# Attention and gated MLP on one core: the same instructions in another written order, with other homes for the ring buffers

## The chip, the cores and the metric

The kernel runs on one core of a Trainium2 chip. A core has four computing engines, TensorE (PE, with its weight load PEld as a row of its own), VectorE (DVE), ScalarE (ACT) and GpSimd (POOL), and SyncE (SP), which here only issues DMAs. Each has an instruction queue that it works off in order; they wait for each other through semaphores. The metric is the device time of one launch in microseconds (us), as the median of several runs.

## The reference

```python
def _attn_ref(q, k, v):                        # q, k, v: (8, 8, 576, 64)
    scores = scale * np.matmul(q, k.transpose(0, 1, 3, 2))
    rel = pos[:, None] - pos[None, :]
    mask = (rel >= 0) & (rel < window)         # window 64
    scores = np.where(mask, scores, -1000000000.0)
    attn = np.exp(scores - np.max(scores, axis=-1, keepdims=True))
    attn = attn / (np.sum(attn, axis=-1, keepdims=True) + 1e-09)
    return np.matmul(attn, v)

def _moe_ref(x, w_gate, w_val, w_out, rms_g):  # x: 4608 x 512, d_ff 1536
    xn = x / np.sqrt(np.mean(x * x, axis=-1, keepdims=True) + 1e-06) * rms_g
    g = xn @ w_gate
    silu = g * (1.0 / (1.0 + np.exp(-g)))
    return silu * (xn @ w_val) @ w_out
```

The output of the attention, 8 x 576 tokens with 8 x 64 features, is the x of the second function.

## The kernel before

**Tiling.** Attention goes by pair of heads: 8 batches of 4 pairs, 32 pairs in all, numbered 0 to 31. The tokens then make nine tiles of 512, t = 0 to 8, and the hidden layer six chunks of 256, c = 0 to 5. A weight or an operand of the MLP is kept as two 16-bit parts (high and low), and a product takes three matmuls: high by high, high by low, low by high.

**Stages.** The pairs of batches 0 and 1 are worked first: loads of `q` (line 660) and `kv` (lines 674, 676), scores `sc` on PE (line 727), mask and maximum on DVE (line 740), exponential on ACT (line 743), scaling on POOL (line 830), transposes `tr` on PE (line 838) with their copies `pt` on DVE and ACT, and values `xp` on PE (line 859). Beside them the weights come in as 64-bit floats and are widened: a staged load `st` (line 502), an exponential `mp`, `mn` on ACT (line 517), a sum `pw` on PE or POOL (lines 527, 523), an or into the bits on DVE (line 531), then scaling by powers of two, with the norms `z` (line 580), and the split in two parts. The root mean square of the first tokens is spread over the partitions by PE (`rb`, line 1277) and taken into `xb` by DVE (line 1305).

Tiles 0 and 1 use plain products `pg` (gate) and `pv` (value) of 12 matmuls of 512 columns each, lines 1397 to 1399; DVE puts them together in `th` (lines 1481 and 1485), which also empties the PSUM bank of the product. Tiles 2 to 8 use a scheme with seven half-size products in place of eight (`product`, line 1700, matmuls of 256 columns), and from tile 3 on the products of the output do too (line 1639). The combined weights of these schemes are made once, put into DRAM (`sevens0` to `sevens5`, one for each chunk, and `outer`) and loaded again for each tile and chunk into two places, `wt0` and `wt1` (lines 1610 and 1620), in three loads for a chunk: one of 128x3072 and two of 128x2048 numbers. A new load into a place waits until the products that read it are done.

The later batches have another way through the attention: scores, then four writes `via<-pm` into DRAM (line 706, one for each quarter of the partitions) and one read `pm<-via` in another layout (line 712), which has to wait until the writes have landed. SP issues these, the loads of `q` and `kv`, the loads of weights and the output (`out<-ot`, lines 1681 and 1893), all in one queue.

**What sets the order.** `SEQUENCE` (lines 44 to 224) is a text of 3894 labels, one for each piece of work: `s01` is a score of pair 0, `m010` a mask, `+g1311.0` a step after a product of tile 1, `.235.3` a step of another kind. The place of a label is its turn. `run_all` emits the pieces in this order, as far as what they need is done, and after it each engine's instructions are bound to the order in which they were written:

```python
AT = {n: k for k, n in enumerate(SEQUENCE.split())}
...
    for ins in traced[start:]:
        if ins.engine in before and ins.engine in WRITTEN(nc):
            tc.add_manual_dep(
                ins, before[ins.engine].name,
```

**Ring buffers.** Tiles of one kind (the `q`, the `kv`, the 512-column scratch `t2k` and a dozen others) share a few buffers. `HOMES` (line 228) says by a digit which buffer the k-th tile of a kind gets; a new tile waits for the readers of the one that was there:

```python
return self.pool.tile(shape, dtype, tag=f"{tag}_{HOMES[tag][k]}", name=name, bufs=1)
```

Of the kernel before, what the change touches and what calls it, by code (L numbers as in the profile page):

```python
# [56 lines left out]
N001 p500 t601 z32 O001 P001 l20 r501 u600 u601 G0101 x30 r500 O000 s70 m700 e411 m701 p410 A010 .229.2 a701 b5 M010 N010 O010 v60 y60 .230.2 p411
r411 a700 i70 w700 x31 G0200 A020 P000 t611 h30 t610 t40 e510 w701 G0211 r410 M020 e511 P010 e600 t41 G0201 d61 t50 G0210 e601 A011 u610 u611 M011 z40
.1 l30 t700 v61 p511 u700 z14 N011 y61 s71 h31 m710 p600 r600 m711 p601 p510 r601 r511 a711 a710 G0300 l31 A021 z41 i71 z42 x41 t701 z33 r510 e620
w710 u701 .26 e621 p621 q6q w711 d64 h40 h41 G0310 t710 G0301 p620 u710 l41 N020 A030 O011 t51 z50 t711 v70 M021 .237.2 b6 M030 N030 N021 r620 u711  # L60
G0311 e610 y70 z43 v71 y71 q7q l40 .234.0 O020 r621 .2 .2.5 .2.7 b7 .2.0 e611 G0400 .2.1 z51 f62 G0410 .2.6 .2.2 A031 M031 .2.11 .2.3 .2.4 d65 p611
P020 N031 O030 .2.9 O021 p610 R1 .2.8 z52 e641 r611 x51 e640 z44 p640 h51 r610 p641 S1 z53 h50 G0401 G0411 O031 A040 f60 l50 r640 B10 F100 F102 .9
H100 e651 e650 .233.0 G0500 r641 d63 F101 G0510 .2.14 A051 B11 H102 f64 M040 N040 F110 l51 F112 G0511 F103 A050 H103 .2.13 F111 F113 M050 f61 P030
.2.10 H101 G0501 N050 P011 p650 e631 z54 p651 r651 .8 .10 L100 P021 A041 M041 r650 H21 N041 .10.7 M051 .10.2 .10.6 L102 L101 e630 f65 .10.5 .2.15 L103
p630 G1000 G1001 r630 N051 .2.12 G1100 O050 P031 G1110 .10.8 p631 r631 f63 L21 .228.3 o0 o1 P050 .2.17 .2.16 .2.18 o2 A110 O040 G1101 h60 .10.1 .17
P040 M110 .2.19 G1011 .228.1 A111 M111 O041 P041 H11 .10.15 .231 .232 G1010 h61 N110 .10.3 .10.4 l60 .10.0 l61 h62 l62 G1111 .10.9 U10 .231.2 h63 N111
.228.4 .2.20 .2.21 L11 H22 .228.5 h64 U30 .228.6 .228.7 .228.10 D3 Ht3 l64 O051 P051 l63 .228.8 .228.9 .2.22 A101 h65 l65 .229.1 D1 Ht1 .231.3 Lt1
A100 M101 .27 M100 D2 Ht2 U31 .231.0 D4 .228.11 Lt3 Ht4 T3 N100 .18 .3 .10.12 .4 O111 .233.2 .46 .5 O100 L22 Lt2 Lt4 N101 P100 .229.3 .229.4 .229.5
# [1946 lines left out]
```

## Time and profile before

| | |
|---|---|
| median of 3 runs | 916.0 us (913.63 to 919.79) |
| span of the profiled execution | 916.2 us |
| PE busy | 893.7 us, 98% |
| PE weight load busy | 686.0 us, 75% |
| DVE busy | 697.3 us, 76% |
| ACT busy | 566.2 us, 62% |
| POOL busy | 454.9 us, 50% |
| DMA | 198.63 MB, mean 217 GB/s |

The rows that are printed further down come from one profiled execution. A row of a timeline has its start in us from the start of the span, the busy time, the engine, the source line and operation, out<-in, the shapes and the count; in brackets the idle time of the engine ahead of it and what ended it. A busy time of a matmul is longer than the step to the next one, since matmuls overlap in the pipeline; the step between starts is what PE needs for one. A row of a window has, for each engine, the busy time and in brackets the number of instructions, and then PE's granted clock as a share of full speed, the mean busy share of the DMA engines and GB/s.

### The profile page before, as it was taken

The page shows a single profiled execution, that of the slowest core. Times are in us where ns is not written, and L with a number is a line of the kernel's source. Part 1 is how long each engine was busy: PE and PEld are TensorE (multiplying, and loading weights), DVE is VectorE, ACT ScalarE, POOL GpSimd, SP SyncE. Part 2 cuts the span into 40 slices and gives each one's busy share as a digit, 9 for nine tenths or more (in the row PEclk, how much of TensorE's full clock was granted, in tenths as well). Part 3 has the DMA queues.
Part 4 walks back from the last instruction along what each step waited for, and adds up shares of the span by engine and source line. Part 5 has one row for each costly group of instructions (what it writes and reads, how often), then busy time and mean ns, then how long its engine had stood idle before and what let it go on. Part 6 is the DMA issues. An engine that isn't in the chain of part 4 may idle for free.

```text
span 916.2 us, 22827 instructions
## 1 busy us (share of the span) xinstructions
PE 893.7 (98%) x8541; PEld 686.0 (75%) x8541; DVE 697.3 (76%) x1916; ACT 566.2 (62%) x1465; POOL 454.9 (50%) x517
## 2 busy tenths in 40 slices
PE   7889999999999999999999998999999999999998
PEld 5644554544558875888888887888888888888887
DVE  6999978786987889898767874789678867724760
ACT  7887785554556566676747665665767555624551
POOL 6467986544355155645543734554547543420440
PEclk9799999999999999999999999999999999999999
DMA  8776642557779875798487757785696556647641
GB/s 325 248 226 211 214 141 61 148 148 216 216 225 308 282 255 157 256 313 276 165 282 269 237 208 236 271 279 193 196 319 219 208 194 213 204 127 233 185 158 47
DMA packets 105439, 198.63 MB, mean 217 GB/s; under 512 B 27760, under 2 KB 64624, under 8 KB 105328
## 3 DMA queue, kind: packets, MB, share of 16 engines
q1 hardware_dynamic: 104752, 195.99, 65.2%
q8 instruction: 67, 1.10, 0.5%
q10 hardware_dynamic: 576, 1.18, 0.3%
q14 instruction: 44, 0.36, 0.1%
HBM read 159.39 MB, written 37.75 MB: 215 GB/s over the span
## 4 chain that ended last, share of the span: by engine, by line
PE 88%; DVE 7%; DMA 2%; issue 1%; ACT 1%; POOL 1%; SPq 0%; ACTq 0%; POOLq 0%; DVEq 0%
PE a L1700 42%; PE o L1639 16%; PE po L1397 3%; PE po L1398 3%; PE po L1399 3%; PE x L902 3%; PE sc L727 3%; PE pv L1397 2%; PE pv L1399 2%; PE pv L1398 2%; PE pg L1397 2%; PE pg L1398 2%; PE pg L1399 2%; DVE p L740 1%; DVE top L568 1%; DMA wt<-sevens 1%
## 5 line engine op out<-in xcount | busy, mean ns | idle before, releaser
L1700 PEld LDWEIGHTS <-wt 128*128 128x128 f16 x3528 | 344.3, 98 | 49.2 <-DMA wt<-sevens 3.5
L1700 PE MATMUL a<-xn,wt 128*128 128x256 f16 x2016 | 236.9, 273 | 0.4 <-POOL xn L1378 0.2
L1700 PE MATMUL a<-wt,wt 128*128 128x256 f16 x1224 | 149.1, 274 | 3.3 <-DMA wt<-sevens 3.3
L1737 ACT ACTIVATE th<-a,hsc 128x256 f32<-128x256 f32 x168 | 78.8, 474 | 105.7 <-DVE a L1801 79.2
L1772 POOL TENSOR_TENSOR h<-th,h 128x512 f16<-128x512 f32 x84 | 98.1, 1179 | 67.5 <-ACT h L1770 61.3
L1772 POOL TENSOR_TENSOR wt<-u,wt 128x512 f16<-128x512 f32 (+1 forms) x72 | 67.1, 935 | 127.6 <-ACT wt L1770 77.1
L1639 PE MATMUL o<-wt,h 128*128 128x256 f16 x864 | 100.4, 273 | 0.0
L1801 DVE TENSOR_TENSOR a<-a,s 128x512 f32<-128x512 f32 x90 | 62.6, 695 | 48.3 <-PE a L1700 35.8
L1732 DVE SCALAR_TENSOR_TENSOR th<-th,a 128x256 f32<-128x256 f32 x168 | 69.6, 414 | 37.5 <-ACT th L1737 37.3
L1639 PEld LDWEIGHTS <-h 128*128 128x128 f16 x864 | 84.1, 98 | 10.7 <-issue 0.5
L743 ACT ACTIVATE pm<-pm,st 128x128 f32<-128x128 f32 (+1 forms) x216 | 83.9, 390 | 12.4 <-DVE st L740 12.2
L698 POOL TENSOR_TENSOR pm<-pm,st 128x512 f32<-128x512 f32 (+1 forms) x72 | 60.6, 870 | 56.6 <-DVE st L772 24.1
L1733 DVE SCALAR_TENSOR_TENSOR th<-a,th 128x256 f32<-128x256 f32 x168 | 71.2, 424 | 5.8
L1639 PEld LDWEIGHTS <-wt 128*128 128x128 f16 x648 | 62.9, 98 | 9.6 <-issue 1.8
L1718 ACT COPY s<-a 128x512 f32<-128x512 f32 x90 | 52.3, 585 | 26.4 <-PE a L1700 24.5
L1770 ACT CAST h<-th 128x512 f16<-128x512 f32 x84 | 51.4, 616 | 10.7 <-DVE th L1733 5.7
L740 DVE CUSTOM_DVE_ANT_0 pm<-sc,blocked 128x128 f32<-128x128 f32 x192 | 48.1, 282 | 6.3 <-PE sc L727 6.1
L1397 PE MATMUL po<-wt,h 128*128 128x512 f16 x136 | 51.6, 379 | 0.0
L1398 PE MATMUL po<-wt,h 128*128 128x512 f16 x136 | 51.5, 379 | 0.0
L1399 PE MATMUL po<-wt,h 128*128 128x512 f16 x136 | 51.5, 379 | 0.0
L727 PE MATMUL sc<-kv,q 64*64 64x128 f32 (+1 forms) x1056 | 43.5, 290 | 7.0 <-DMA q<-q 6.0
L1639 PE MATMUL o<-wt,wt 128*128 128x256 f16 x432 | 49.8, 273 | 0.0
(239 smaller groups left out, 1772.2 us busy)
## 6 DMA issues: line engine op xcount, KB each, us to landing
wt<-sevens SPq DMA_DIRECT2D x84, 512.0 KB, 5.5
wt<-sevens SPq DMA_DIRECT2D x42, 768.0 KB, 5.8
wt<-outer SPq DMA_DIRECT2D x24, 768.0 KB, 6.0
kv<-kv SPq DMA_DIRECT2D x28, 608.0 KB, 5.0
via<-pm SPq DMA_DIRECT2D x96, 144.0 KB, 2.8
pm<-via SPq DMA_DIRECT2D x24, 576.0 KB, 5.8
q<-q SPq DMA_DIRECT2D x28, 288.0 KB, 5.6
st<-w_gate SPq DMA_DIRECT2D x6, 1024.0 KB, 5.9
```

What stands on the lines that cost most here:

```text
L727: nc.tensor.matmul(out.rearrange("p (n c) -> p n c", c=D), lhsT=qt[hd, j * D : (j + 1) * D], rhs=halves[hd, :1, :] if j == 0 else halves[h ...
L743: nc.scalar.activation(part, part, AF.Exp, bias=low, scale=-1.0, accum_out=total)
L1397: nc.tensor.matmul(acc, lhsT=lh, rhs=rh, start=first, stop=False)
L1398: nc.tensor.matmul(acc, lhsT=lh, rhs=rl, start=False, stop=False)
L1399: nc.tensor.matmul(acc, lhsT=ll, rhs=rh, start=False, stop=last)
L1639: nc.tensor.matmul(acc[:, sub * HT : (sub + 1) * HT], lhsT=l[:, x, sub * P : (sub + 1) * P], rhs=r[:, y, :], start=first and c == cs[0] an ...
L1700: nc.tensor.matmul(acc[:, i * HT : (i + 1) * HT], lhsT=ws[l][:, kt, :], rhs=b[:, m, kt, :], start=at_start, stop=kt == 1 and j == 2, skip_ ...
L1732: nc.vector.scalar_tensor_tensor(cols, cols, 1.0, acc[:, :HT], ALU.add, ALU.mult)
L1733: nc.vector.scalar_tensor_tensor(cols, acc[:, HT:], 2.0**-42, cols, ALU.mult, ALU.mult)
L1737: nc.scalar.activation(cols, acc[:, :HT], AF.Tanh, scale=th_scale[:, c : c + 1])
L1772: nc.gpsimd.tensor_tensor(lo, src, hi, ALU.subtract)
L1801: nc.vector.tensor_tensor(to, acc, kept.pop((c, name)), ALU.add)
```

## The change

Only two tables are replaced. `SEQUENCE` has the same 3894 labels in another order: a label moves by 24 places on average, the farthest by 518 forward and 649 back. `HOMES` gives other buffers to the tiles of the rings, in numbers that fit the new order. The code, the instructions and their sizes are the same. A line of the text and the start of the line of `HOMES`, as samples:

```diff
-q0 k0 s01 m010 q2 s00 k1 q1 s10 a010 m011 a011 j1 j0 m000 c11 i01 a000 m001 w010 m100 q3 k2 m101 a001 a101 i00 w011 a100 j2 s20 t010 c01 c20 s11 m200
+q0 k0 s01 q1 q2 m010 m011 k1 k2 j1 a010 a011 s00 m000 a000 i01 m001 q3 w010 s10 a001 s20 w011 s11 m100 a100 i00 m101 a101 j0 t010 m200 t011 c11 m201
...
-HOMES = {'q': '01202102101000121021012102102010',
+HOMES = {'q': '10210020212020101220101002012210',
```

What this does to the engines' queues is seen at three places. The first is PE's queue at the start, around the scores of pair 5 (`sc_5`, two pieces `sc_5_0` and `sc_5_1`) and the broadcast `rb` of the first tokens. Before:

```order
L1076 MATMUL tot_0_320_710<-consts_85,ssq_0_558 128x1 x2
L727 MATMUL sc_5_0_0_719<-kv_5_610,q_5_687 64x128
L727 MATMUL sc_5_0_1_720<-kv_5_610,q_5_687 64x128
...
L1277 MATMUL rb_0_0_742<-ident_74,rm_0_698 128x128 x2
L1277 MATMUL rb_0_0_742<-ident_74,rm_0_698 128x64
L727 MATMUL sc_5_1_0_754<-kv_5_610,q_5_687 64x128
L727 MATMUL sc_5_1_1_755<-kv_5_610,q_5_687 64x128
...
L1277 MATMUL rb_0_0_742<-ident_74,rm_0_698 128x128
L1277 MATMUL rb_0_0_742<-ident_74,rm_0_698 128x64
L1277 MATMUL rb_0_512_775<-ident_74,rm_0_698 128x64
L838 MATMUL tr_4_0_1_784<-ident_74,p_4_0_1_605 128x128 x2
```

The same place in the changed kernel:

```order
L1277 MATMUL rb_0_512_741<-ident_74,rm_0_701 128x64
...
L1277 MATMUL rb_0_0_757<-ident_74,rm_0_701 128x128 x2
L1277 MATMUL rb_0_0_757<-ident_74,rm_0_701 128x64
L1277 MATMUL rb_0_0_757<-ident_74,rm_0_701 128x128
L1277 MATMUL rb_0_0_757<-ident_74,rm_0_701 128x64
L727 MATMUL sc_5_1_0_765<-kv_5_628,q_5_626 64x128
L727 MATMUL sc_5_1_1_766<-kv_5_628,q_5_626 64x128
...
L838 MATMUL tr_4_0_0_776<-ident_74,p_4_0_0_610 128x128 x2
```

All of `rb` now stands ahead of the scores of pair 5, and of these `sc_5_1` comes first. On ACT's queue, which issues the first loads of queries, the order `q_0`, `q_2`, `q_1` has become `q_0`, `q_1`, `q_2`.

The second place is on PE as well, later in the start: the products of tile 0, `pg_0_3` (gate, number 3) and `pv_0_2` (value, number 2), of 12 matmuls each, of which the first three stand here. Before:

```order
L1397 MATMUL pg_0_3_1193<-xn_0_741,wt0_69 128x512
...
L1398 MATMUL pg_0_3_1193<-xn_0_741,wt0_69 128x512
...
L1399 MATMUL pg_0_3_1193<-xn_0_741,wt0_69 128x512
...
L576 MATMUL n2_3_1227<-sq_3_1213,one_82 128x2
...
L1397 MATMUL pv_0_2_1253<-xn_0_741,wt0_69 128x512
...
L1398 MATMUL pv_0_2_1253<-xn_0_741,wt0_69 128x512
```

In the changed kernel:

```order
L576 MATMUL n2_3_1225<-sq_3_1200,one_82 128x2
...
L1397 MATMUL pv_0_2_1227<-xn_0_756,wt0_69 128x512
...
L1398 MATMUL pv_0_2_1227<-xn_0_756,wt0_69 128x512
...
L1399 MATMUL pv_0_2_1227<-xn_0_756,wt0_69 128x512
...
L1397 MATMUL pg_0_3_1285<-xn_0_756,wt0_69 128x512
```

The value product comes ahead of the gate product now.

The third place is SP's queue where tile 4 ends and tile 5 begins: the weights of chunk 0 (`wt0<-sevens0`) and of chunk 1 (`wt1<-sevens1`) for tile 5, the way of pair 24 through DRAM, and output of tile 4. Before:

```order
L1610 DMA wt0_69<-sevens0_119 128x3072
L1610 DMA wt0_69<-sevens0_119 128x2048
L1681 DMA out<-ot_4_0_1_7593 128x256 x2
L706 DMA via_24_7603<-pm_24_7261 32x4x288 x4
L1610 DMA wt1_70<-sevens1_120 128x3072
L712 DMA pm_24_7261<-via_24_7603 128x1152
L1610 DMA wt0_69<-sevens0_119 128x2048
L1681 DMA out<-ot_4_0_0_7693 128x256 x2
```

In the changed kernel:

```order
L1610 DMA wt0_69<-sevens0_119 128x3072
L1610 DMA wt0_69<-sevens0_119 128x2048 x2
L706 DMA via_24_7673<-pm_24_7229 32x4x288 x4
L660 DMA q_27_7682<-q 128x576
L1610 DMA wt1_70<-sevens1_120 128x3072
L1681 DMA out<-ot_4_0_1_7635 128x256 x2
L712 DMA pm_24_7229<-via_24_7673 128x1152
L1681 DMA out<-ot_4_1_1_7670 128x256 x2
L1610 DMA wt0_69<-sevens2_121 128x3072
```

The third load of `sevens0` has moved from behind `pm_24<-via_24` to a place ahead of `via_24<-pm_24`; the first load of `sevens2` now follows behind `pm_24<-via_24` and an output.

## Rows read from the trace of the kernel before

**Rows 1.** The page: span, and busy time of each engine with its share.

```profile
span 916.2 us, 22827 instructions
PE 893.7 (98%) x8541; PEld 686.0 (75%) x8541; DVE 697.3 (76%) x1916; ACT 566.2 (62%) x1465; POOL 454.9 (50%) x517
```

**Rows 2.** Timeline of PE, matmuls of 512 and of 256 columns.

```profile
342.55 0.38 PE L1397 MATMUL po<-wt,h 128*128 128x512 f16 x1
342.77 0.38 PE L1398 MATMUL po<-wt,h 128*128 128x512 f16 x1
...
561.68 1.47 PE L1700 MATMUL a<-wt,wt 128*128 128x256 f16 x12
```

**Rows 3.** Windows: the start, its slow part, the middle, the rest.

```profile
core 0: us, PE busy (x) PEld busy (x) DVE busy (x) ACT busy (x) POOL busy (x), PEclk, DMA share, GB/s
0.00:80.00 80.00, 65.90 (x668) 43.13 (x669) 70.13 (x288) 66.47 (x183) 45.51 (x83) 0.91 0.76 260
30.00:50.00 20.00, 14.92 (x144) 11.63 (x145) 18.02 (x79) 16.56 (x38) 8.58 (x13) 0.69 0.85 288
80.00:565.00 485.00, 483.98 (x4440) 339.21 (x4440) 397.82 (x1073) 309.56 (x824) 263.13 (x276) 1.00 0.68 218
580.00:916.00 336.00, 332.08 (x3320) 294.20 (x3318) 221.43 (x539) 184.46 (x443) 145.37 (x158) 1.00 0.62 205
```

**Rows 4.** Timeline of ACT at the end: the last output copy.

```profile
912.38 0.69 ACT L1674 ACTIVATE ot<-o,hsc 128x512 f32<-128x512 f32 x1 [2.51 <-PE o L1639]
```

**Rows 5.** Timeline of DVE in the start: three waits and the step at 80 us.

```profile
5.76 0.29 DVE L740 CUSTOM_DVE_ANT_0 p<-sc,blocked 128x128 f32<-128x128 f32 x1 [3.84 <-PE sc L727]
...
9.53 0.29 DVE L740 CUSTOM_DVE_ANT_0 p<-sc,blocked 128x128 f32<-128x128 f32 x1 [0.83 <-PE sc L727]
...
45.45 0.94 DVE L1305 SCALAR_TENSOR_TENSOR xb<-xb,gsb_late,rb 128x512 f32<-128x512 f32 x2 [1.17 <-PE rb L1277]
...
80.05 0.68 DVE L1485 SCALAR_TENSOR_TENSOR th<-pv,th 128x512 f32<-128x512 f32 x1
```

**Rows 6.** Timeline of PE in the start: the second scores, and the products after 80 us.

```profile
8.20 2.68 PE L727 MATMUL sc<-kv,q 64*64 64x128 f32 x40 [1.55 <-DMA q<-q]
...
81.12 0.38 PE L1397 MATMUL pv<-xn,wt 128*128 128x512 f16 x1
```

**Rows 7.** Timeline of PE around 565 us.

```profile
562.99 2.78 PE L1700 MATMUL a<-xn,wt 128*128 128x256 f16 x24
569.04 4.16 PE L1700 MATMUL a<-wt,wt 128*128 128x256 f16 x24 [3.27 <-DMA wt<-sevens]
```

**Rows 8.** Window from 570 to 580 us, columns as in rows 3.

```profile
570.00:580.00 10.00, 10.00 (x103) 8.13 (x102) 6.77 (x16) 5.23 (x16) 0.92 (x1) 0.83 0.47 152
```

**Rows 9.** Timeline of SP's queue ahead of that wait.

```profile
554.46 1.78 SPq L706 DMA_DIRECT2D via<-pm  x4
556.34 0.40 SPq L1610 DMA_DIRECT2D wt<-sevens  x1
559.94 0.34 SPq L712 DMA_DIRECT2D pm<-via  x1
560.33 0.43 SPq L1610 DMA_DIRECT2D wt<-sevens  x1
```

**Rows 10.** The chain of waits there: start, us, what it was spent on.

```profile
555.80 4.08 DMA via<-pm
559.94 0.34 SPq L712
...
560.33 8.67 DMA wt<-sevens
```

**Rows 11.** DMA issues, KB, median us to landing: whole span, 556:570, 740:900.

```profile
wt<-sevens SPq DMA_DIRECT2D x84, 512.0 KB, 5.5
...
wt<-sevens SPq DMA_DIRECT2D x2, 768.0 KB, 6.2
wt<-sevens SPq DMA_DIRECT2D x3, 512.0 KB, 8.7
...
wt<-sevens SPq DMA_DIRECT2D x22, 512.0 KB, 4.5
```

**Rows 12.** Windows of light and of dense weight loading, columns as in rows 3.

```profile
140.00:160.00 20.00, 20.00 (x96) 9.22 (x95) 17.06 (x48) 11.31 (x25) 12.74 (x11) 1.00 0.18 43
...
860.00:880.00 20.00, 20.00 (x185) 17.93 (x184) 15.03 (x35) 11.64 (x24) 8.11 (x8) 1.00 0.56 165
```

More of the change, by code (lines that the diff above doesn't have):

```diff
@@ new lines @@
++u247.3 +u255 +u244 .63 +u234.1.0 .240.4 +u247.1 .78 +u233.0 +u256 +u247.1.0 +u255.0 +u252.1 +u252.2 .66.21 +u253 +u234.2 .240.5 .66.22 +u252.2.0
++u244.1 .78.0 +u256.0 .78.1 +u244.1.0 .78.2 +u253.1 +u253.2 +u244.2 +u234.3 +u237.3 +u244.3 .240.6 .240.7 .67 +u234.0 +u257 +k220 +k221 +u253.2.0
++u257.0 .85 +u257.2 .69 +u257.1 .68 .78.3 +u243.0 +u257.1.0 .241.0 .70 .241.1 +k222 +u254 .86 .71 .241.2 .72 .86.2 .78.5 .241.4 +u254.1 +u254.1.0
+.86.0 .240.8 .86.3 .241.3 .86.6 .86.1 .78.6 .86.7 .242.0 .78.4 +k223 .86.5 +k224 .73 .73.8 .86.8 .73.0 .241.5 .86.11 .241.6 +u257.3 .241.7 +u254.2
@@ new lines @@
+.171.20 +u523.0 .164 +u504.6 +u517.7 +u532.0 +u514.2 .180.18 +u537 +u545 +u542 +u533.1 +u527.6 .165 +u533.2 +u533.2.0 +u527.4 +u514.4 +u527.5 .166
++u537.0 +u537.1 +u545.0 +u524.1.0 .180.19 +u527.8 +u527.7 +u551 +u546 +u543 .167 +u524.2 +u524.4 +u546.0 .171.21 +u524.0 +u534 .171.22 +u542.1
++u537.1.0 +u537.2 +u537.4 +u543.0 +u537.3 .168 +u542.2 +u534.1 +u555 +u547 +u533.0 +u514.3 +u543.1 +u551.0 +u537.6 +u537.8 +u514.5 .180.20 +u552
++u534.1.0 +u543.1.0 .198 +u542.2.0 +u547.0 +u537.5 +u537.7 +u514.6 +u556 +u555.0 .172 +u547.1 +u556.0 .174 +u524.3 +u542.0 .180.21 .180.22 +u524.5
@@ new lines @@
++u727.3 +u733.1 +u727.6 +u733.2 +u733.2.0 +u737.0 +u732.0 +u723.0 +u742 +u714.4 +u727.8 +u714.6 +u737.1 +u742.1 +u714.3 +u737.1.0 +u737.2 +u704.5
++u714.5 +u745.0 +u704.4 +u751 +u751.0 +u724.3 +u737.3 +u737.6 +u755 +u746 +u743 +u734 +u746.0 +u724.0 +u733.0 +u747 .227.9 +u742.2 +u727.5 +u752
++u704.6 +u737.8 +u724.5 +u727.7 +o720 +u756 +u743.0 +u743.1 +u742.2.0 +u743.1.0 +u747.0 +u747.1 +u755.0 +u753 +u724.2 +u724.4 +u737.4 +u747.1.0
++u747.2 +u734.0 +u734.1 +u747.3 +u752.0 +u742.0 +u747.6 +u752.1 +u744 +u734.1.0 +u752.2 +u756.0 +u737.5 +u734.3 +u752.2.0 +u753.0 +u747.4 +u753.1
@@ new lines @@
++u757 +u747.8 +u737.7 +u753.1.0 +u757.0 +u747.5 +u747.7 .227.7 +u744.1 +u757.1 +o710 +u757.1.0 +u757.2 +u744.1.0 +o711 +u757.3 +u754 +u744.2 +u757.6
+.227.8 +u757.8 +u757.4 +u734.2 +u757.5 +u744.3 +u754.1 +o750 +o751 +u757.7 +u744.0 +u754.1.0 +u754.2 +u734.5 +o712 +o712.0 +o752 +u754.4 +u754.6
++u734.4 +u724.6 +o752.1 +o721 +o760 +o761 +u754.3 +o762 +u754.5 +u734.6 +u744.5 +u744.4 .227.10 +o762.2 +o730 +o762.0 +o752.0 +u754.0 +u744.6 +o731
++o732 +o770 +o722 +o771 +o772 +o722.0 +o732.0 +o732.1 +u805 +o772.1 +o772.2 +u802 +u801 +u801.0 +u805.0 +o740 +o762.1 +o772.0 +o741 +u803 +u806
@@ L224 @@
++o831 +o832 +o832.0 +o870 +o871 +o872 +o821 +u854.5 +o832.1 +u844.3 +u844.5 +o822 +o872.1 +o840 +o822.0 +o822.1 +o872.2 +o841 +o842 +o862.1 +o842.0
++o852.0 +o842.1 +o862.0 +o872.0 +o822.1.0 +o872.2.0 +o832.1.0 +o842.2 +o842.2.0
 """
```

340 lines of the change are left out of this document (161 added, 179 removed).

## Prediction

> **What bounds the kernel now.** I read the page first, then the windows of each stage, then the timelines around the few places where the tensor engine stands. The span is 916.2 us and PE is busy for 893.7 of it, DVE for 697.3 [rows 1]. A busy PE is not yet a PE without room, so its timeline comes next: one 128x512 matmul follows the other after 0.22 us (342.55, 342.77), and 12 matmuls of 256 columns start at 561.68 and are followed at 562.99, after 1.31 us, which is 0.109 us each [rows 2, 7]. Half the columns take half the time, so PE is streaming columns and a new order cannot make it faster; it can only remove time in which PE stands or has the slow clock.
>
> The windows say how much of that there is [rows 3]. From 80 to 565 us PE is idle 485.00 − 483.98 = 1.0 us. From 580 to the end it is idle 336.00 − 332.08 = 3.9 us, nearly all of it after the last matmul: the last output copy of ACT runs at 912.38 and its store lands after it [rows 4]. In the first 80 us PE is idle 14.1 us, and its granted clock is 0.91 on average, 0.69 between 30 and 50 us, where 20 us at 0.69 lose 6.2 us of full speed. There DVE sets the pace: it is busy 70.13 of 80 us, idle 9.87. Its timeline [rows 5] shows 3.84 of the idle before the first scores, 0.83 at 9.53 (again waiting for scores) and 1.17 at 45.45 (waiting for the broadcast `rb`). At 80.05 it works `pv_0_1` into `th` (line 1485, 0.68 us); this empties the bank that product `pv_0_2` writes, and PE starts that product at 81.12 [rows 6].
>
> One more place is left, 565 to 580 us. PE waits 3.27 us for a `wt<-sevens` load, until 569.04, and from 570 to 580 the granted clock is 0.83: ten microseconds at 0.83 are 1.7 us lost [rows 7, 8]. SyncE's timeline [rows 9] and the chain [rows 10] say why the load is late. SyncE's queue is in order. At 554.46 it issues the four `via<-pm` transfers of attention pair 24, at 556.34 one `wt1<-sevens1`; then `pm<-via` must wait until the `via` writes have landed (4.08 us after 555.80), so it goes out at 559.94, and the third `wt0<-sevens0` load stands behind it, at 560.33. That load then takes 8.67 us.
>
> **The change, part by part.** The instructions are the same ones, so no duration is added or removed; what counts is the three places.
>
> *The late stall.* In the new order both small `wt0<-sevens0` loads stand right behind the large one and ahead of `via_24<-pm_24`. Counting PE's new order from the last product that reads the old `wt0` to the first that reads this load, some 18 us of matmuls (0.109 us per 256 columns) lie between; the load took 8.67. So the stall is gone: −3.3, and with it the slow clock after it: −1.7. That the clock's loss goes with the stall I take from [rows 7, 8] alone, since in the other 485 us without a stall the clock is 1.00 [rows 3]. [...]
>
> *What is late next.* I went through the new order for every load and counted the PE work between the instruction that frees its place (with all that stands ahead of it on SyncE's queue) and the product that needs it: the cover. The shortest are 6.55 us (60 products of 256 columns; tile 8), three of 7.86 us (72 products) and four of about 8.4. In the old order, loads with covers of 6.55 and 7.86 us caused no wait, as the 1.0 us idle of [rows 3] shows. These loads land in 5.5 us as a median, in 8.7 from 556 to 570 us, where the `via` transfers and two of 768 KB overlap with three of them, and in 4.5 between 740 and 900 us [rows 11], where the shortest cover lies. Lower bound 0: all land as before. Upper bound: all land in 8.67, and the waits are 8.7 − 6.55 = 2.1, three times 0.8 and four times 0.3, in all 5.6 us, and 1.7 of clock behind the one wait of any length. I take +0.5, near the lower end, because the covers of the old order held.
>
> *The start.* DVE's own work up to the end of this line-1485 step is, added up in the new order with the mean durations of the old trace, 71.3 us in place of 70.9 (70.13 until 80.00 and the 0.73 to its end). But product `pg_0_3`, 12 matmuls of 512 columns or 12 × 0.218 = 2.6 us (0.218 is twice the 0.109 of 256 columns), stood ahead of `pv_0_2` on PE and now stands behind it. PE gets to this point in step with DVE, whose step releases it, so what it did ahead of the step is now still to do behind it: +0.4 and +2.6 = +3.0 if DVE idles as before. Two of its idle pieces should go. `q_1` moves from third to second on ACT's queue ahead of `q_2`: the second score product waited 1.55 us at 8.20 for its q [rows 6], and DVE 0.83 behind it. And all of `rb_0` now stands ahead of the scores of `sc_5`; in the old order `sc_5_0` came before it and `sc_5_1` inside it, which is where DVE waited 1.17. That is −2.0, and the start costs +1.0. Bounds: of the idle 9.87 only the 3.84 before the first scores stays, −6.0 + 3.0 = −3.0; or nothing is saved and one more wait like the 1.55 comes, 3.0 + 1.55 = +4.6, for `kv_5` now takes the place of `kv_2`, free later, and only 5.7 us of PE work in place of 8.2 cover its way to the scores. The slow clock between 30 and 50 us costs nothing more where DVE sets the pace.
>
> *The end.* Three output tiles of tile 8 are now stored one behind the other ahead of the last one. The last copy and store remain: between 0 and the 0.5 us of some short issues, +0.3.
>
> Sum on the profiled execution: 916.2 − 3.3 − 1.7 + 0.5 + 1.0 + 0.3 = 913.0. The median of the runs is 916.0, 0.2 lower, so **912.8 us** as median.
>
> **The rivals.**
> - *The new order starves on other loads* (slower than before). Place: the eight thin covers above. For it: the same load took 8.67 us at 560.33 [rows 10], in a stretch where SyncE's transfers crowd, and the new order moves loads together. Against it: median 5.5, and equal covers held. Price: 5.6 + 1.7 in place of the 0.5: 919.6 us. With the landing L for the four thinnest, (L − 6.55) + 3 (L − 7.86) + 1.7 eats the other 3.7 us of gain from L = 8.0 on. If each of the eight waits drew its own 1.7 of slow clock, 12 us more, 931.
> - *The stall only moves.* In the new order the `wt0<-sevens2` load stands behind `pm_24<-via_24`, with a cover of 9.8 us; 4.08 + 0.39 + 8.67 = 13.1 would be 3.3 too much, and the time would be 912.8 + 3.3 + 1.7 = 917.8. With the median landing it is 10.0, a wait of 0.2.
> - *The start costs its upper bound*: 912.8 + 3.6 = 916.4, no change.
> - *The start gains its lower bound*: 912.8 − 4.0 = 908.8; if PE gains back some of the 6.2 us of slow clock as well, below 906.
> - *PE has room after all.* Its weight loads are busy 75% of the span [rows 1], 9.22 of 20 us from 140 us on and 17.93 from 860 us on [rows 12]. If that were the measure, the 485 us of [rows 3] with 339.21 could shrink to 339.21 / 0.90 = 377, a time near 808. The spacing of [rows 2] speaks against it: nothing lies between matmuls even where weight loading is light. [...]
>
> **How the numbers follow.** Forecast 0.46; thin covers 0.14 (0.05 of it with repeated slow clock, over 925); the stall moves 0.06; start dear 0.11 (0.01 over 925); start cheap 0.13 (0.06 below 907); room on PE 0.01; something that I have not seen 0.05 below 907 and 0.04 above 925. About 1%, or 9 us, is what a measurement can tell here, with runs from 913.6 to 919.8. Faster by more than that (below 906.8) has 0.06 + 0.01 + 0.05 = 0.12, slower (above 925.2) 0.05 + 0.01 + 0.04 = 0.10, the same 0.78. The range goes from the cheap start, 908.8 less some clock, 906, to the thin covers, 919.6 and a little, 921, which leaves out 2 in 10; the forecast's own range is 910 to 916.
>
> **What would show it.** Right: no wait of PE over 1 us for `wt<-sevens` between tiles 4 and 5, granted clock 1.00 there; DVE's work up to the line-1485 step ahead of `pv_0_2` about 71 us with idle near 8; that step ending at 79 to 80 us; PE idle under 2 us from 80 us to the last matmul. Wrong: rows of PE with a long idle and `DMA wt<-sevens` as releaser at the thin covers, a clock under 1.00 behind them; DVE idle 10 us or more ahead of that step, or waits of PE for `kv` or `q` at `sc_5`. The sum would be wrong as a whole if the first 80 us follow not DVE but the loads, or if a row shows PE's 256-column matmuls at other than 0.109 us.

## The result, and the profile after

The changed kernel takes **922.06 us** as the median of eight runs (920.73 to 925.04), the kernel before, beside it, 915.68 (913.63 to 919.79): 1.007 times as long, with an interval of 1.0051 to 1.0089. It is 6.4 us slower, still within 1%, and above the range of 906 to 921. The late stall is gone from the profile as forecast; the loss comes from the start: DVE's step at 80 us ends 5.2 us later, and product `pg_0_3` is still to do behind it.

The page and the windows of the changed kernel, as in [rows 1] and [rows 3] (PE, PEld, DVE, ACT, POOL busy with their instructions, granted clock, DMA share, GB/s):

```profile
span 920.0 us, 22750 instructions
PE 893.2 (97%) x8536; PEld 685.9 (75%) x8541; DVE 698.1 (76%) x1916; ACT 562.8 (61%) x1465; POOL 448.0 (49%) x517
```

```profile
core 0: us, PE busy (x) PEld busy (x) DVE busy (x) ACT busy (x) POOL busy (x), PEclk, DMA share, GB/s
0.00:80.00 80.00, 58.19 (x612) 40.10 (x616) 65.41 (x279) 60.17 (x173) 41.23 (x77) 0.83 0.68 234
80.00:565.00 485.00, 483.83 (x4402) 334.20 (x4403) 401.01 (x1080) 309.90 (x818) 261.00 (x279) 1.00 0.70 220
565.00:580.00 15.00, 15.00 (x165) 13.31 (x163) 7.11 (x16) 9.44 (x28) 6.44 (x9) 1.00 0.84 280
...
10.00:15.00 5.00, 1.65 (x11) 1.09 (x9) 4.84 (x32) 4.93 (x26) 4.04 (x8) 0.89 1.05 385
...
15.00:25.00 10.00, 9.66 (x104) 7.02 (x106) 5.58 (x32) 5.52 (x18) 6.02 (x12) 0.54 0.58 214
```

From 80 us on PE does not stand any more than before: it idles 1.17 us up to 565, none from 565 to 580, and the clock is 1.00 in these windows. In the first 80 us PE is busy 58.19 in place of 65.90 and DVE 65.41 in place of 70.13. The same two short stretches of the kernel before show where:

```profile
10.00:15.00 5.00, 4.96 (x61) 3.19 (x54) 4.47 (x36) 4.21 (x23) 4.52 (x9) 1.00 1.05 385
15.00:25.00 10.00, 8.96 (x140) 6.53 (x141) 9.36 (x50) 10.00 (x33) 6.23 (x13) 1.00 0.76 275
```

Between 10 and 15 us PE now has 11 matmuls in place of 61; then it is busy 9.66 of 10 us and gets through 104 where it did 140, at a clock of 0.54, and DVE, which I had taken for the pacemaker, stands 4.42 us. PE's timeline of the changed kernel:

```profile
4.75 5.36 PE L727 MATMUL sc<-kv,q 64*64 64x128 f32 x92 [4.75 <-DMA q<-q]
...
12.13 0.77 PE L838 MATMUL tr<-ident,p 128*128 128x128 f32 x5 [1.25 <-POOL p L830]
15.30 0.90 PE L838 MATMUL tr<-ident,p 128*128 128x128 f32 x3 [2.40 <-POOL p L830]
16.13 1.13 PE L727 MATMUL sc<-kv,q 64*64 64x128 f32 x16
...
25.32 0.67 PE L727 MATMUL sc<-kv,q 64*64 64x128 f32 x16
...
35.97 0.38 PE L576 MATMUL n<-sq,one 128*128 128x2 f32 x2 [3.04 <-DVE sq L572]
```

All 92 first scores now run without a pause, until 10.1 us; PE then stands 1.25 and 2.40 us, because the next rows of its queue are transposes whose `p` POOL has not yet scaled. In this execution the granted clock falls within the second wait (0.50 from 14 to 15 us). From then on 16 scores take 1.13 us, at 25.32 again 0.67. What they wait for, on POOL and DVE:

```profile
13.94 0.61 POOL L1036 COPY wt<-kv 64x512 f32<-64x512 f32 x1
14.63 0.62 POOL L830 TENSOR_TENSOR p<-p,st 128x256 f32<-128x256 f32 x1
```

```profile
12.93 0.19 DVE L824 RECIPROCAL st<-st 128x5 f32<-128x5 f32 x1
...
16.24 0.42 DVE L845 COPY pt<-tr 128x256 f32<-128x256 f32 x1 [0.75 <-PE tr L838]
17.43 0.29 DVE L740 CUSTOM_DVE_ANT_0 p<-sc,blocked 128x128 f32<-128x128 f32 x1 [0.57 <-PE sc L727]
...
85.30 0.67 DVE L1485 SCALAR_TENSOR_TENSOR th<-pv,th 128x512 f32<-128x512 f32 x1
```

The scaling follows masks, maxima and a reciprocal on DVE, which are as late as before (reciprocals at 12.93 and 15.30, in the kernel before at 13.15 and 15.27); only the scores were early. POOL's copy of `kv` (0.61 us) stands between two scalings in both kernels. The line-1485 step of `pv_0_1`, at 80.05 in [rows 5], is at 85.30.

### The profile page after: what moved, and what is told of

Read it like the earlier page. It is cut to its first block, busy times and chain, and to the rows that moved or that the text cites. A ratio compares the mean times of both kernels' runs of the same rounds, so it can differ in the third digit from the quotient of the medians.

```text
span 920.0 us, 22750 instructions
## 1 busy us (share of the span) xinstructions
PE 893.2 (97%) x8536; PEld 685.9 (75%) x8541; DVE 698.1 (76%) x1916; ACT 562.8 (61%) x1465; POOL 448.0 (49%) x517
## 4 chain that ended last, share of the span: by engine, by line
PE 94%; DVE 2%; POOL 1%; DMA 1%; issue 1%; ACT 0%; SPq 0%; POOLq 0%
PE a L1700 42%; PE o L1639 18%; PE sc L727 4%; PE po L1397 3%; PE po L1398 3%; PE po L1399 3%; PE x L902 3%; PE pg L1397 2%; PE pg L1399 2%; PE pg L1398 2%; PE pv L1397 2%; PE pv L1399 2%; PE pv L1398 2%; PE xp L859 1%; PE tr L838 1%; PE rb L1245 1%
## 5 line engine op out<-in xcount | busy, mean ns | idle before, releaser
L1700 PE MATMUL a<-wt,wt 128*128 128x256 f16 x1224 | 146.1, 273 | 0.0
L1733 DVE SCALAR_TENSOR_TENSOR th<-a,th 128x256 f32<-128x256 f32 x168 | 71.3, 424 | 5.8
L727 PE MATMUL sc<-kv,q 64*64 64x128 f32 x1056 | 43.2, 293 | 4.8 <-DMA q<-q 4.8
```

The lines of the kernel that those rows point to most:

```text
L727: nc.tensor.matmul(out.rearrange("p (n c) -> p n c", c=D), lhsT=qt[hd, j * D : (j + 1) * D], rhs=halves[hd, :1, :] if j == 0 else halves[h ...
L1700: nc.tensor.matmul(acc[:, i * HT : (i + 1) * HT], lhsT=ws[l][:, kt, :], rhs=b[:, m, kt, :], start=at_start, stop=kt == 1 and j == 2, skip_ ...
L1733: nc.vector.scalar_tensor_tensor(cols, acc[:, HT:], 2.0**-42, cols, ALU.mult, ALU.mult)
```

## The experiments

A kernel with labels of both orders takes the named labels first, in the one order, and then all others in the other; its ring buffers have homes dealt anew for the mixture. Each time stands beside runs of the kernel before on the same chip. A run's time is its span and 1.7 to 2.3 us, about 1.8 for the kernel before and 1.9 for the changed one.

### Which part of the order

**`start_old_rest_new`**: the first 520 labels of the order before, the rest as in the changed kernel.

```diff
- SEQUENCE = new
+ SEQUENCE = old[:520] + [l for l in new if l not in old[:520]]
```

> The first 520 labels (the start, up to the products of tile 0) stand in the order of before, the other 3374 in the order of the change; homes follow each. Theory A (the loss is made in the start): DVE busy near 70 of the first 80 us again, no waits of 2 us of PE for POOL's p at 12 to 16 us, no stall at 565 us; about 913 us, 9 below the changed kernel. Theory B (the loss is made after 80 us, by loads or homes): it stays near 922.

914.57 us against 915.03, ratio 0.9997 (0.9978 to 1.0016). The new order from about 80 us on costs nothing and gains nothing that can be measured; the 7.5 us between this kernel and the changed one (6.7 by the two ratios) lie in the start. Its span is 912.3, that of the changed kernel 920.0: 7.7.

**`start_new_rest_old`**: the same with the two orders exchanged.

```diff
- SEQUENCE = new
+ SEQUENCE = new[:520] + [l for l in old if l not in new[:520]]
```

> The mirror image: the first 520 labels in the order of the change, the rest in the order of before. Theory A: before's 915.7 plus about 8.8, so 924, with the waits of PE at 12 to 16 us and the clock of 0.5 behind them. Theory B: near 916.

922.48, ratio 1.0075 (1.0046 to 1.0105). The new start alone brings the whole loss.

**`first300_old`** and **`first300_new`** cut at 300 labels.

```diff
- SEQUENCE = new
+ SEQUENCE = old[:300] + [l for l in new if l not in old[:300]]
```

```diff
- SEQUENCE = new
+ SEQUENCE = new[:300] + [l for l in old if l not in new[:300]]
```

> Only the first 300 labels (about 27 us) in the order of before, the rest in the order of the change. Theory A1 (two pieces of lost DVE time: 3.7 us from 10 to 25 us, 1.9 us from 45 to 55 us): the first piece comes back, 922.1 - 3.7 = 918.4, and DVE has done about 17.6 us of work at 25 us instead of 14.6. Rival A2 (DVE idle costs nothing here, the whole loss is the order of products against DVE's work later in the start): 922.

> The mirror image: the first 300 labels in the order of the change, the rest in the order of before. Theory A1: 915.7 + 3.7 = 919.4, with DVE at 14.6 us of work at 25 us. Rival A2: 916.

`first300_old` took 918.27, 1.0034 (1.0014 to 1.0054), as theory A1 had it, but by luck. In its profile the start loses nothing up to 40 us; what it loses is a wait at the border of the two orders, with a granted clock of 0.70 from 60 to 70 us:

```profile
65.72 0.69 PE L829 MATMUL tr<-ident,p 128*128 128x128 f32 x2 [2.55 <-POOL p L821]
```

So it does not say that half of the loss lies behind label 300, and `first100_old` below, with fewer labels put back, is the faster one. `first300_new` missed: 932.03, 1.0174 (1.0134 to 1.0213). Its timeline of PE shows a wait that neither order has, at the border of the two:

```profile
70.49 0.37 PE L850 MATMUL xp<-pt,wt 128*64 128x64 f32 x1 [5.07 <-ACT pt L836]
```

So neither kernel says how the start's loss divides; a cut has to be judged by its own trace as well.

**`first100_old`**: only the first 100 labels in the old order. 95 labels are among the first 100 of both, so that nearly the same work stands there, in another order.

```diff
- SEQUENCE = new
+ SEQUENCE = old[:100] + [l for l in new if l not in old[:100]]
```

> Only the first 100 labels (about 12 us) in the order of before, the rest in that of the change. If what starts the loss is the early scores with nothing behind them for PE (they stand in these labels): as first300_old, 918.4, with clock 1.00 from 15 to 25 us. If the loss comes from what follows (copies and products from 12 to 27 us): 922.

915.93 against 915.11, 0.9989 (0.9968 to 1.001): with 100 labels put back, 6 of the 6.4 us are gone. (It still has `pg_0_3` behind `pv_0_2`, and no late stall; by the sizes below these two about cancel.) Its windows:

```profile
10.00:15.00 5.00, 4.12 (x51) 2.54 (x46) 4.48 (x33) 4.59 (x24) 4.31 (x9) 1.00 1.06 398
15.00:25.00 10.00, 8.67 (x135) 6.14 (x135) 9.44 (x52) 9.56 (x31) 6.37 (x12) 1.00 0.76 267
```

PE works through, the clock is 1.00, DVE is busy 9.44 of 10. From label 101 on this kernel has the order of the changed one, so I can put the same pieces of work side by side. For each piece I took the end of its last instruction on DVE, ACT or POOL and subtracted its end in `first100_old`; a row is the median over pieces that stand at these places of the new order:

```
places     at us   after  new_look2  new_side  s21_early  warm15b  warm15b_side
20-60       13.4   -0.13      -0.10     -0.11       0.01    -0.44         -0.11
60-100      18.9    2.53       2.56      2.56       1.50     0.73          1.06
100-140     24.3    3.97       4.12      3.44       2.86     0.34          0.68
140-180     30.5    4.12       4.20      3.70       3.02     0.64          0.97
180-220     40.1    5.09       5.26      4.91       3.98     2.40          5.26
350-400     78.2    5.08       5.26      5.56       4.01     1.82          5.25
700-900    184.5    5.07       5.25      5.55       4.01     1.81          5.26
2400-3000  601.1    5.79       6.03      5.09       3.50     1.65          4.77
```

The changed kernel ("after", and two more executions of it, `new_look2` and `new_side`) is level until 13 us, 4.0 us late at 24, 5.1 late at 40, and then nothing catches up (5.8 at 601). There are two steps: 4.0 us in the stretch of the slow clock, and 1.0 between 31 and 40 us, which the next runs bring out.

**`new_look2`**, **`old_look2`** and **`new_side`** are the changed kernel and the kernel before, unaltered, once more.

> A second execution of the changed kernel. If the half clock from 15 to 24 us belongs to this order and not to one execution: 0.50 again there, DVE near 14.6 us of work at 25 us, span 919 to 921.

> A second execution of the kernel before. Theory S (the stall at 565 us comes in some executions only, those of 918 us and more): if it is timed at 913 to 915, no wait of PE over 1 us for sevens between 550 and 580 us; if at 918 or more, the wait and the clock of 0.83 behind it are there again.

> The changed kernel beside warm15b_side on the same chip: its 922.1 over before's 915.7 again, that is 1.007 of it; warm15b_side 2.9 us below it if holding the clock is worth what the profiles show, 0 to 1.5 below if not.

The first has a span of 921.1, with waits of 1.12 and 2.40 us where the profile above has 1.25 and 2.40; `new_side` has 1.74 and 2.16 and takes 923.26 (1.0079, 1.0049 to 1.0108). So the gap belongs to the order, not to one execution. `old_look2` is told below.

### The waits, the clock, and one small operation

**`s21_early`** puts the scores `sc_2_1` (label `s21`) ahead of the transposes (`t100`) that PE waits for.

```diff
- w200 t100 u100 w201 a111 d00 s21 a110
+ w200 s21 t100 u100 w201 a111 d00 a110
```

> The changed kernel with one label moved: the scores of pair 2's second piece (s21) stand ahead of the transposes of pair 1 (t100), so that PE has 1.1 us of work in the 2.40 us in which it waits for POOL. Theory C: the gap is cut to 1.3 us, DVE finds its next scores ready and does not wait 0.57 us for them; if the clock also stays up, 919 to 920, if not 921. Rival W: POOL's step at 15.2 us is still the one that PE waits for next: 922.

921.88, 1.0077 (1.0048 to 1.0106): no gain that can be measured. The waits are 1.80 and 1.22 us now, and the clock falls all the same, to 0.60 on average from 15 to 25 us. In the table this kernel is 3.0 us late where the changed one is 4.1.

**`warm15`** and **`warm15b`** leave the order alone and give PE 128x128 matmuls to do while it waits; nothing reads their result, and the kernel's own work is complete. `warm15` has 5 and 10 calls behind the labels `t011` and `t001`, `warm15b` 2 and 4:

```diff
+         for _ in range({'t011': 2, 't001': 4}.get(label, 0)):
+             spare = banks.tile([P, TT], F32, tag=f"bank{free_banks[0]}", name=f"spare_{label}_{_}")
+             nc.tensor.matmul(spare[:, :P], lhsT=ident, rhs=ident, start=True, stop=True, skip_group_check=True)
```

> The changed kernel with 15 more matmuls of the identity with itself into a free PSUM bank, 5 behind tr_0_1_1 and 10 behind tr_0_0_1, where PE stands idle for 1.25 and 2.40 us; their results are not read. Theory C (the clock carries the loss): granted clock near 1.00 from 15 to 25 us instead of 0.50 and 0.59, DVE idle in these 10 us down from 4.4 to 2 us or less, time 919 or lower. Rival W (the wait for POOL itself carries it, whatever the clock): clock 1.00, but DVE as idle as before, and 922.

> As warm15, but sized by its trace: an added matmul took 0.53 us there, not 0.21, and ten of them kept PE busy until 19.2 us, past POOL's release at 15.1. Now 2 behind tr_0_1_1 (1.1 us for the 1.25 us gap) and 4 behind tr_0_0_1 (2.1 us for the 2.40 us gap), results not read. Theory C (the clock carries the loss): clock near 1.00 from 15 to 25 us, PE's next transposes at 15.3 us as before, DVE's work at 25 us up from 14.55 to 16.5 or more, time 922 - 2.5 = 919.5. Rival W: clock 1.00 but DVE near 14.6 at 25 us, and 922.

`warm15` took 925.16 (1.01; 1.0076 to 1.0125). I had the size wrong: one such matmul call takes 0.53 us on PE, so ten of them held it until 19.2 us, and DVE waited 3.62 us for the transposes behind them. With the right number, `warm15b`, the timeline of PE and the windows are:

```profile
10.07 0.93 PE L396 MATMUL spare_t<-ident 128*128 128x128 f32 x4
11.97 0.77 PE L841 MATMUL tr<-ident,p 128*128 128x128 f32 x5 [0.97 <-POOL p L833]
12.58 2.02 PE L396 MATMUL spare_t<-ident 128*128 128x128 f32 x8
15.14 0.55 PE L841 MATMUL tr<-ident,p 128*128 128x128 f32 x3 [0.54 <-POOL p L833]
15.62 0.67 PE L730 MATMUL sc<-kv,q 64*64 64x128 f32 x16
```

```profile
10.00:15.00 5.00, 3.40 (x20) 2.21 (x17) 4.84 (x32) 4.93 (x27) 4.04 (x8) 1.00 1.06 395
15.00:25.00 10.00, 9.26 (x149) 6.47 (x149) 8.91 (x51) 8.90 (x27) 6.55 (x14) 1.00 0.76 273
```

The transposes begin at 15.14, hardly ahead of the 15.30 of the changed kernel, since POOL is no faster; but the clock stays at 1.00, 16 scores take 0.67, and DVE is busy 8.91 of 10 us in place of 5.58. In the table the kernel is 0.3 us late at 24 us, not 4.0. This settles the mechanism of the first step: the wait for POOL itself costs 0.3 us, the slow clock behind it 3.6. Yet the time is 921.99, 1.0055 (1.0034 to 1.0076), almost no better. `warm15b_look2`, `warm15b_look3` and `warm15b_side` are the same kernel again, the last beside `new_side`; they were to tell why.

> A second execution of warm15b. In its first one the clock stayed at 1.00 from 10 to 30 us and DVE had done 18.02 us of work at 25 us, yet its runs have a median of 921.99. If the added matmuls hold the clock in every execution: 18 us of DVE work at 25 us again, and a span near 917.6. If the clock falls in other executions all the same: below 1.00 from 15 to 25 us, DVE near 15, span near 920.

> A third execution of warm15b, with the same two outcomes as the second: clock 1.00 from 10 to 30 us with 18 us of DVE work at 25 us, or a clock that falls there and about 15.

> warm15b and the changed kernel timed side by side on one chip. Three profiled executions of warm15b had spans of 917.1 to 917.9, two of the changed kernel 920.0 and 921.1, so 2.9 us less; the medians of two different calls were 922.0 and 922.1. If the profiled executions stand for all: 2.9 us less than new_side. If the gain exists in some executions only: 0 to 1.5 less.

The first two have spans of 917.9 and 917.1, like the first one's 917.6, against 920.0, 921.1 and 919.3 of the changed kernel. `warm15b_side` took 921.45 (1.0061; 1.004 to 1.0081) beside 923.26 of `new_side`, 1.8 us less, half of the 3.6 at 24 us; its profiled execution, with a span of 920.6, held its clock too (1.00 from 10 to 30 us), and lost what it had gained at another place. Its DVE, POOL and PE:

```profile
31.12 0.40 DVE L848 COPY pt<-tr 128x256 f32<-128x256 f32 x1
31.46 3.77 DVE L575 TENSOR_TENSOR sq<-top 128x2 f32<-128x2 f32 x1
35.15 0.28 DVE L743 CUSTOM_DVE_ANT_0 p<-sc,blocked 128x128 f32<-128x128 f32 x1
```

```profile
30.23 1.40 POOL L1048 TENSOR_TENSOR ssq<-ssq,kv 128x576 f32<-128x576 f32 x1
31.59 1.15 POOL L526 TENSOR_TENSOR wt<-mp,mn 128x512 f32<-128x512 bf16 x1
32.70 1.39 POOL L1048 TENSOR_TENSOR ssq<-ssq,kv 128x576 f32<-128x576 f32 x1
34.06 1.15 POOL L526 TENSOR_TENSOR wt<-mp,mn 128x512 f32<-128x512 bf16 x1
```

```profile
35.28 0.59 PE L579 MATMUL n<-sq,one 128*128 128x2 f32 x2 [5.49 <-DVE sq L575]
```

A square of 128x2 elements is on record for 3.77 us, until 35.23; POOL's last operation ends at 34.06 + 1.15 = 35.21. The same square in the changed kernel and in `first100_old`, with POOL beside it:

```profile
34.60 1.31 DVE L572 TENSOR_TENSOR sq<-top 128x2 f32<-128x2 f32 x1
...
33.38 1.40 POOL L1045 TENSOR_TENSOR ssq<-ssq,kv 128x576 f32<-128x576 f32 x1
34.74 1.15 POOL L523 TENSOR_TENSOR wt<-mp,mn 128x512 f32<-128x512 bf16 x1
```

```profile
30.48 0.19 DVE L572 TENSOR_TENSOR sq<-top 128x2 f32<-128x2 f32 x1
...
29.25 1.40 POOL L1045 TENSOR_TENSOR ssq<-ssq,kv 128x576 f32<-128x576 f32 x1
30.62 1.15 POOL L523 TENSOR_TENSOR wt<-mp,mn 128x512 f32<-128x512 bf16 x1
```

Each time the square ends 0.02 us behind the end of a POOL operation, within the rounding of the rows: of `ssq` at 30.65 in `first100_old`, of the `wt<-mp,mn` behind it at 35.89 in the changed kernel, of the next `wt<-mp,mn`, two operations later, at 35.21 in `warm15b_side`. All 20 traces fall into these three: the nine whose first 100 labels are in the old order (two of them with `q_1` and `q_2` exchanged) have 0.19 to 0.26 us, nine of the eleven others 1.30 or 1.31, and two, `warm15` and `warm15b_side`, 3.77. That is the second step of the table: 1.0 us in the changed kernel, 4.3 in `warm15b_side` (from 0.97 to 5.26), of which the longer square itself is 3.77 − 0.19 = 3.6; it uses up all that the clock had saved. That the square waits for POOL is read from these ends; no run moved POOL's operations away from it, so it is not shown by experiment. The rows also show POOL operations that started after the square and ended before it: one in the changed kernel (34.74), three in `warm15b_side` (31.59, 32.70 and 34.06). Nothing in my sum moved on POOL.

### Other terms of the prediction

**`pg3_late`**: the kernel before, with product `pg_0_3` (label `G0110`) moved behind `pv_0_2` (`G0101`), as in the new order.

```diff
- t600 x21 w601 G0110 r401
+ t600 x21 w601 r401
...
- u601 G0101 x30
+ u601 G0101 G0110 x30
```

> The kernel before with one label moved: product pg_0_3 stands behind pv_0_2. The prediction's term: DVE releases pv_0_2, so the 2.6 us of pg_0_3 are added: 915.0 + 2.6 = 917.6. Rival: PE has 2.6 us of slack against DVE there, and nothing changes: 915.

920.09 against 916.3, 1.0036 (1.0013 to 1.0058): 3.8 us of the medians, for a term of 2.6. The order costs what I said or more, but the size is not clean. Its PE timeline:

```profile
79.73 0.38 PE L527 MATMUL pw<-mp,unit 128*128 128x512 bf16 x1 [1.89 <-ACT mp L517]
...
82.10 0.63 PE L1398 MATMUL pv<-xn,wt 128*128 128x512 f16 x1
82.53 0.63 PE L1399 MATMUL pv<-xn,wt 128*128 128x512 f16 x1
```

Where `pg_0_3` stood, PE now waits 1.89 us for ACT, and `pv_0_2` behind it begins with matmuls 0.43 us apart in place of 0.22 (granted clock 0.70 from 80 to 85 us): eight of them take 3.4 us in place of 1.7. It is the pair of the start again, cover taken from a wait and a slow clock behind it. The changed kernel, with 1.00 there, does not pay these 1.7 us; an estimate of the term without them is 3.8 − 1.7 = 2.1.

**`joined_q1`**: `start_old_rest_new` with the load `q_1` ahead of `q_2`, the one edit of the new start that was to gain.

```diff
- s01 m010 q2 s00 k1 q1 s10
+ s01 m010 q1 s00 k1 q2 s10
```

> start_old_rest_new with one label pair exchanged: q_1 is loaded ahead of q_2. The prediction's step on it: PE's wait of 1.33 us for q at 8.05 us and DVE's 0.8 us behind it go, 914.6 - 0.8 = 913.8. Rival: PE runs ahead and then waits for POOL as the changed kernel does, and nothing is gained or it gets slower.

914.91, 0.9992 (0.9976 to 1.0008), no gain over `start_old_rest_new`. PE's timeline shows what took the place of the wait:

```profile
9.15 1.33 PE L727 MATMUL sc<-kv,q 64*64 64x128 f32 x20 [1.23 <-DMA kv<-kv]
```

The `q` is there, and the `kv` that follows it is not. The saving of 0.83 that I gave this edit was only the next wait.

**`joined_warm`**: the same with three added matmuls behind `t311`.

```diff
+         for _ in range({'t311': 3}.get(label, 0)):
+ ...
```

> joined_q1 with 3 added matmuls (1.6 us, results not read) behind tr_3_1_1, where PE stands idle for 1.96 us ahead of the values of pair 3. If the half clock from 36 to 48 us costs DVE its idle 1.7 us from 40 to 45 us: clock above 0.9 there, DVE 4.5 of 5 us, and 914.9 - 1.2 = 913.7. If DVE's wait there is for other work: the same 914.9.

914.04, 0.9966 (0.9945 to 0.9986), 0.9 below `joined_q1` in median, less than these runs can tell apart. In its profiled execution PE had waited 1.82 us for `kv` already at 9.69, and the clock was 0.61 from 10 to 15 us; the added matmuls lie elsewhere, so this run decides nothing on them. It does show the slow clock with the old start: 0.68 from 15 to 25 us, with DVE busy 7.58 of the 10 us where `joined_q1` has 1.00 and 9.41.

**`sevens_early`**: the kernel before, with the third `wt0<-sevens0` load (`+o462.1`) right behind the second, ahead of the `via` transfers.

```diff
- +u434.5 +o462.0 +o432.1
+ +u434.5 +o462.0 +o462.1 +o432.1
...
- .150.21 +o462.1 .171.11
+ .150.21 .171.11
```

> The kernel before with one label moved: the third load of sevens0 for tile 5 is issued behind the second, ahead of the way of pair 24 through DRAM, as in the changed kernel. The prediction's term: 3.3 + 1.7 less, 915.5 - 5.0 = 910.5. Rival S (the stall comes in some executions only, as it was absent in start_new_rest_old, whose order there is that of before): 0 to 2.5 less, 913 to 915.5, and no stall in the profile.

913.92 (911.88 to 916.46) against 915.11 (912.64 to 920.82), 0.9968 (0.9949 to 0.9986). This one edit is faster than the kernel before, by 1.2 us of the medians and 2.9 by the ratio, and its profile has no wait for `sevens`. `old_look2`, the kernel before once more, shows why it is not 5: in that execution it had no stall. The window from 560 to 580 us, columns as above:

```profile
560.00:580.00 20.00, 20.00 (x211) 17.73 (x209) 13.79 (x41) 13.39 (x39) 8.03 (x13) 1.00 0.88 323
```

Its span was 912.7, 3.5 under the 916.2 of [rows 1]. Of the 35 runs of the kernel before beside it 13 lie above 917, and none of the 12 of `sevens_early`. That the 13 are the runs with a stall is likely, but only two executions of that kernel have a trace. Of the three other traces with the old order at this place `first300_new` shows the wait (3.08 us), `pg3_late` a short one (0.59) and `start_new_rest_old` none.

## Why the prediction was wrong, step by step

**PE has no room in the middle, DVE's work to the `pv_0_1` step is 71.3 us, `pg_0_3` costs 2.6.** The first two held: the window up to the end of that step, 85.97 us, has DVE busy for 71.35. `pg3_late` measured 3.8 (1.2 to 5.3) for the third, with a spell of slow clock in it; 2.6 lies within, and no run shows it cleanly.

**DVE's idle in the start (the step that failed).** I let DVE idle 9.87 less 2.0. It idles 85.97 − 71.35 = 14.6, well beyond the 10 us that I had named as a sign of being wrong. With the measured idle my own sum comes out: DVE's work +0.5, its idle 14.6 − 9.9 = +4.7, `pg_0_3` +2.6 as forecast, together +7.8, where the spans of the changed kernel and of `start_old_rest_new` differ by 7.7. My term was +1.0 and my upper bound +4.6. Three things went wrong in it.
- I took DVE for the pacemaker all the way and wrote, of the stretch from 30 to 50 us, that the slow clock "costs nothing more where DVE sets the pace". For 10 us in the new order PE sets the pace: at a granted clock of 0.54 it is busy 9.66 of 10 us with transposes, scores and values, and DVE 5.58. The clock's loss was a term of its own, 3.6 of the 4.0 us that are lost by 24 us. What the slow clock costs between 30 and 50 us stays open.
- I searched the new order for waits on loads and counted what came sooner. The first scores did come sooner (no wait of PE for `q` at 8.20, no wait of DVE at 9.53); but with no score left to fill in, PE had to stand at the next piece that waits for the slowest chain, mask, reciprocal, scaling on POOL. Work moved ahead of a wait is cover taken from behind it.
- The bound for one more wait was 1.55, the nearest row. A wait there has a price of its own: 3.65 us of standing, then the slow clock (0.54 from 15 to 25 us). [rows 7, 8] had shown this very pair at 565 us, and I used it only there.

**Of the small steps,** the saving at 45.45 did not come: DVE waits 0.76 for `rb` at 52.24, and 0.36 at 50.21, in place of 1.17. `kv_5` caused no wait at `sc_5`; the expected danger was at the wrong place. No term covered the square that ends with POOL's operations, 1.0 us. And the clock of 0.91 that I read for the first 80 us is too high: it counts the first 13.9 us, of which the trace has no clock record, as full speed, where the rows are slow (last section).

**The late stall.** The mechanism was right: in the changed kernel the three `sevens0` loads go out together at 550.33, ahead of `via`,

```profile
550.33 1.39 SPq L1610 DMA_DIRECT2D wt<-sevens  x3
...
556.66 1.79 SPq L706 DMA_DIRECT2D via<-pm  x4
```

and the clock stays at 1.00. In the profiled executions the stall is worth what I said: beside `old_look2`, which has none, the same pieces of work in the kernel before end 1.4 us earlier at 540 to 560 us and 3.7 later at 575 to 600, which is 5.1 for my 5.0. But I took 5.0 off a median in which, by the runs above 917, most executions do not pay it. I set the sum beside the span, 916.2, and saw the median only 0.2 away; the profiled run's own time is its span and about 1.8, 918.0, and so it lay 2.3 above the median of 915.68. `sevens_early` puts the gain at 1.2 to 2.9, and the whole new order from 80 us on, `start_old_rest_new`, at 0.5, nothing measurable.

**Thin covers and the tail.** PE idles 1.17 us between 80 and 565 and nothing from 565 to 900, with a clock of 1.00, so the rival on thin covers is out. The last copy of ACT begins 920.0 − 916.22 = 3.8 us ahead of the end, as in [rows 4] (916.2 − 912.38 = 3.8): the tail cost nothing.

In sum: start +7.5 by the medians in place of +1.0, the rest −0.5 in place of −4.2; that is 10.2 us of error in two terms. Together the two give +7.0; the change measured +6.4, and these runs cannot tell the 0.6 between them.

## What to carry to other kernels

Where PE works in bursts behind another engine's chain of work, ask of a new order not only what comes sooner but where PE will stand next and for how long, and price the slow clock behind that wait (here 3.6 us) for every engine that is fed by PE. Take a profiled stall for what it is worth on average only after a second execution has shown it too. And look at what runs on POOL beside VectorE's operations, even the tiny ones: the 128x2 square took 0.19 us in `first100_old` and 3.77 in `warm15b_side`.

## What the runs showed of the hardware

- After waits of 1.25 and 2.40 us between 10.0 and 15.3 us, in the second of which the granted clock fell, PE worked at a granted clock of 0.50 until about 24 us; six added matmul calls, 0.93 and 2.02 us of work, kept it at 1.00 (`warm15b`, 10 to 25 us). In `pg3_late` a wait of 1.89 us was followed by 0.70 from 80 to 85 us, in `joined_warm` one of 1.82 by 0.61 from 10 to 15 us. These waits were for POOL, for ACT and for a DMA in turn. The price in the changed kernel fell on DVE: 4.4 us of idle in the 10 us from 15 to 25.
- In the kernel before, early scores are as slow, though its window from 10 to 15 us says 1.00:

```profile
11.43 1.13 PE L727 MATMUL sc<-kv,q 64*64 64x128 f32 x16
...
13.77 0.71 PE L727 MATMUL sc<-kv,q 64*64 64x128 f32 x16
```

  Its trace holds no record of the clock ahead of 13.90 us (10.47 in the changed kernel), and a window counts time without a record as full speed. There the rows' own durations are the measure.
- The 128x2 square on DVE near 30 to 35 us took 0.19 to 0.26, 1.30 to 1.31 or 3.77 us by which POOL operation it ended behind, and 3.77 against 1.30 occurred in one and the same kernel (`warm15b`).
- The late stall came and went between executions of an unaltered kernel: 3.27 us of waiting in `before`'s profile, none in that of `old_look2`.
